# A scan and mixture-of-experts kernel: chunk scale from a Gram matrix, second round of slots after chunk 3, 163 output tiles, another order

## The chip, the cores and the metric

The kernel runs on one core of a Trainium2 chip. A core has TensorE (PE), VectorE (DVE), ScalarE (ACT), GpSimd (POOL) and SyncE (SP), which run their own instruction streams and meet at semaphores, and 16 DMA engines that move data between HBM and the two on-chip memories, SBUF and PSUM. The metric is the device time of one launch in microseconds; the time of a version is the median of its runs.

## The reference

A gated linear recurrence over 4 sequences of 5056 tokens with 256 features gives 20224 rows of 256 values. Each row goes to the one of 8 experts with the largest gate logit, through that expert's two-layer network, and is scaled by its softmax share and by a sigmoid.

```python
log_a = c * sig_r * np.log(np.clip(a_base, 1e-06, 1.0 - 1e-06))[None, None, :]
a_t = np.exp(log_a)
x_gated = np.sqrt(np.maximum(1.0 - a_t * a_t, 1e-06)) * sig_i * x
for t in range(S):
    h = a_t[:, t] * h + x_gated[:, t]
    y[:, t] = h
...
logits = x @ w_gate                    # x: the 20224 rows of y
e_idx = np.argmax(logits, axis=1)
for e in range(E):
    mask = e_idx == e
    h = np.maximum(x[mask] @ w1[e], 0.0)
    out[mask] = gate_w[mask, None] * eom[mask, e, None] * (h @ w2[e])
```

## The kernel before

Tokens come in 21 chunks: chunks 0 and 1 hold 4 tiles of 128 tokens each, chunks 2 to 19 hold 8, chunk 20 holds 6. For a chunk, in blocks of 4 tiles, SP loads the three inputs, ACT and DVE make decay and gated input, and DVE runs the scan (L685). Then the states are cut into two half-precision parts, which needs a power-of-two scale. In chunks 0 and 1 the states are turned into rows by PE (`project`, L719) and each row gets a scale of its own, from a maximum that DVE takes over the PSUM tile (`top`, L733 to L738). From chunk 2 on one scale serves the whole chunk: DVE takes the largest value per feature (`peak`, L771), spreads it over a diagonal (`spread`, L778 and L780), PE sends it to all partitions (`cast`, L784) and DVE makes the scale (`level`, L789 to L793). SP then turns the two parts into rows with a DMA transpose (`flip`, L823), PE computes logits (L831), DVE picks the expert and counts positions (L942), and POOL scatters each tile's rows to the experts' regions in HBM (`scatter_rows`, L427).

The expert network works in slots. A slot is 128 or 256 rows of one expert: SP fetches the rows transposed (L1073), PE runs the first layer into `ph` (L1129), ACT and DVE cut its output into two parts `h` (L1144, L1147), PE runs the second layer into `po` (L1186), ACT scales the result (L1198), POOL stores 128 rows per instruction (L1201). With three products per layer a slot of 128 rows is 48 matmuls of 128 columns and 24 of 256; a slot of 256 rows is 96 of 256 columns. The table SETS says after which chunk each expert gets a slot, and how wide: a *round* is the 8 slots of one chunk. An expert with fewer new rows than its slot holds takes old rows again, and these are not stored. Rows that are over after the last round go into ENDS slots of 128 rows, whose expert is found on the chip; should these not be enough, a loop adds 9 at a time.

The weights of an expert are loaded and cut into two parts by ACT and DVE (`unit`, L548 and L558) during the first chunks. Two Gram matrices per expert on PE (L507) give their scales.

PE, ACT and DVE get their instructions from a planner (`in_order`), which sorts the work by ranks and by assumed durations; the tables of ranks at the head of the file and the `time` arguments of `work` set the order, and each engine runs its own list strictly in that order. SP's and POOL's instructions are issued in the same order. From chunk 3 on a scatter also waits for the ReLU (L1144) that the planner put last before it, so that scatters are spread in time.

Of the kernel before, what the change touches and what calls it, by code (L numbers as in the profile page):

```python
# [7 lines left out]
F32 = mybir.dt.float32  # L8
# [9 lines left out]
P = 128  # L18
# [7 lines left out]
SETS = {1: 128, 2: 128, 4: 128, 5: 128, 6: 128, 8: 128, 9: 128, 10: 128, 11: 128, 13: 256, 15: 256, 17: 256, 19: 256}  # L26
# [5 lines left out]
ENDS = 29  # L32
# [22 lines left out]
LAG = 0.00132  # L55
ALONE = (0, 1, 3, 6)
QUICK = -11.495
ROOT = -24.122
EARLY = -672.359
UNIT_RANK = (509.634, 423.588, 415.962, -121.889, 422.863, 543.847, 40.166, 546.044, 522.559, 567.262, -167.684, 542.792, -125.616, -161.472, 40.642, -115.487)  # L60
CHUNK_RANK = (-672.139, -298.533, 527.534, 84.515, 462.374, 144.822, 553.848)
SLOT_RANK = (-52.797, -70.553, 319.009, -156.421, -51.418)
FILL = -114.953
LOAD_RANK = -17.21
# [158 lines left out]
def rglru_moe(ctx: ExitStack, tc: tile.TileContext, x, r_gate, i_gate, a_param, wg, wog, w1, w2, out, shape):  # L223
# [7 lines left out]
    assert D == 2 * P and E == 8 and F == 8 * P and N % P == 0 and N + (FILLS + 1) * P <= REGION and max(SETS.values()) <= FILLS * P  # L231
# [220 lines left out]
    undo = const.tile([P, 2, E], F32, name="undo")  # L452
# [6 lines left out]
    def unit(u, staged):  # L459
# [58 lines left out]
        def bits():  # L518
            pn = tiles["pg", u][:, P:P + 1]
            nc.vector.tensor_scalar(sc, pn.bitcast(I32), 25, 23, op0=ALU.logical_shift_right, op1=ALU.logical_shift_left)  # L520
            nc.vector.tensor_scalar(sc, sc, -1.0, float((168 - TOP, 172)[i] << 23), op0=ALU.mult, op1=ALU.add)
# [77 lines left out]
    def chunk(c):  # L599
# [102 lines left out]
        rused, row_at = [], []  # L702
        lows, flips = [], []
        for b in range(0, nt, 4) if c < BY_PE else ():
            nb = min(4, nt - b)
            iu = blocks[b // 4][6]
            group = []
            for j in range(b, b + nb):
                pool = "ps_h" if c < len(FIRST) and j % 4 > 1 else "ps_r"
                pu, pold = rings[pool].new()  # L710
                row_at.append(len(rings["rows"].tiles) % ROWS)
                used, old = rings["rows"].new()
                rused.append(used)

                def project(j=j, pool=pool):
                    pf = tiles["prow", c, j] = (ps_h if pool == "ps_h" else ps_r).tile([P, 512], F32, name=f"prow_{c}_{j}", tag=pool)
                    H = tiles["it", (c, j // 4 * 4)]
                    for h in range(ND):
                        nc.tensor.matmul(  # L719
                            pf[:, h * P:(h + 1) * P + 2 * E], lhsT=H[:, h, (j % 4) * P:(j % 4 + 1) * P],  # L720
                            rhs=iw[:, h, :], start=h == 0, stop=h == ND - 1, skip_group_check=True,
                        )

                def pr(j):
                    return tiles["prow", c, j][:, 0:ND * (P + 2 * E)].rearrange("p (h d) -> p h d", h=ND)[:, :, 0:P]

                def r4(j):
                    return rows_all[:, row_at[j], 0:META].rearrange("p (k h d) -> p k h d", k=2, h=ND)

                def top(js, pr=pr):  # L730
                    am, sc = st("am", 1), st("sc", 1, I32)
                    for j in js:
                        nc.vector.tensor_reduce(am[:, j, :], pr(j), axis=AX.XY, op=ALU.max, apply_absolute_value=True)  # L733
                    js = slice(js[0], js[-1] + 1)
                    nc.vector.tensor_scalar(
                        sc[:, js, :], am[:, js, :].bitcast(I32), 0x7F000000, 0x7F000000, op0=ALU.bitwise_and, op1=ALU.bitwise_xor
                    )
                    nc.vector.tensor_scalar(  # L738
                        sc[:, js, :], sc[:, js, :], float(TOP - 1 << 23), float(0x7F000000), op0=ALU.add, op1=ALU.min
                    )  # L740

                def hi(j=j, pr=pr, r4=r4):
                    sc = st("sc", 1, I32)[:, j, :].bitcast(F32)
                    if c < len(UPPERS) and UPPERS[c] == "D":
                        nc.vector.tensor_scalar(r4(j)[:, 0], pr(j), sc, None, op0=ALU.mult)
                    else:
                        nc.scalar.activation(r4(j)[:, 0], pr(j), AF.Copy, scale=sc)

                def lo(j=j, pr=pr, r4=r4):
                    nc.vector.tensor_copy(st("lz", 2 * E)[:, j, :], tiles["prow", c, j][:, P:P + 2 * E])  # L750
                    nc.vector.scalar_tensor_tensor(
                        r4(j)[:, 1], pr(j), st("sc", 1, I32)[:, j, :].bitcast(F32), r4(j)[:, 0], op0=ALU.mult, op1=ALU.subtract
                    )

                w = work("PE", 0.49, project, [states[b // 4], pold, gates], EARLY + c / 100, uses=[pu, iu], slack=SLACK[c > 4])
                group.append((j, w, pu, old, used, hi, lo))
                if len(group) == TOPS or j == b + nb - 1:
                    js = [v[0] for v in group]
                    t = work(
                        "DVE", 0.385 * len(js) + 0.22, lambda js=js, f=top: f(js), [v[1] for v in group] + chain["small"],  # L760
                        tail_rank + TAIL, uses=[v[2] for v in group],
# [79 lines left out]
        if c >= BY_PE:  # L841
# [6 lines left out]
            for blk in blocks:  # L848
                pus.append(rings["ps_r"].new())
# [422 lines left out]
    with tc.manual_schedule(engines=engines):  # L1272
        for w in in_order([w for w in works if not w.late], {"DVE": 3.0, "ACT": 3.0}):
            w.emit()
# [43 lines left out]
```

## Time and profile before

| | |
|---|---|
| median of 3 runs | 1047.06 us (1043.95 to 1047.54) |
| the profiled execution | 1041.86 us, span 1040.2 us |
| PE, weight loads | 945.2 us busy (91%), 871.8 us (84%) |
| DVE, ACT, POOL | 708.7 us (68%), 623.7 us (60%), 365.5 us (35%) |
| mean granted TensorE clock | 0.955 |

Busy time is an average over stages. Matmul and weight load overlap, so a busy PE is read as "PE had work", and what a slot costs is read from the distance between the same places of two slots that follow each other. The granted clock is a share of full speed: 1.0 is 2.4 GHz, 0.5 is 1.2 GHz.

### The profile page before, as it was taken

Reading aid. Unit: us, or ns where it says so; the run is one execution under the profiler, and the core shown is the slowest. Engines: PE = TensorE matmul, PEld = TensorE weight load, DVE = VectorE, ACT = ScalarE, POOL = GpSimd, SP = SyncE. Lnnn points to the kernel's source line nnn. Section 1 sums busy time; section 2 is a strip of 40 time slices with the busy share of each in tenths; the row PEclk is TensorE's granted clock in tenths of the full one; section 3 lists DMA queues with packets and bytes.
Section 4 is the critical chain, followed back from the end, with each engine's and each line's share of the span. In section 5 each row is a group of like instructions: output and inputs, shape, how many; then the busy total and the mean of one; then the engine's idle time right before and its main releaser. Section 6 shows DMA issues by size and latency. Waiting matters only on the chain.

```text
span 1040.2 us, 29569 instructions
## 1 busy us (share of the span) xinstructions
PE 945.2 (91%) x11462; PEld 871.8 (84%) x11462; DVE 708.7 (68%) x1798; ACT 623.7 (60%) x931; POOL 365.5 (35%) x341
## 2 busy tenths in 40 slices
PE   2449549999999989999999999999999999999996
PEld 2438449989989989899999888888888889999996
DVE  4988998999889888888888888885222222342231
ACT  6977886788678677768778788532232322333332
POOL 1120522553555444544445455443212122111111
PEclk8658869999999999999999999999999999999999
DMA  9997678999999999989999899766122212788971
GB/s 328 382 274 168 196 202 191 211 220 209 222 235 217 209 239 242 181 195 215 243 199 226 211 220 212 142 153 185 51 52 52 52 47 97 233 245 235 254 232 44
DMA packets 274447, 200.82 MB, mean 193 GB/s; under 512 B 213725, under 2 KB 224735, under 8 KB 274305
## 3 DMA queue, kind: packets, MB, share of 16 engines
q1 hardware_dynamic: 248224, 139.89, 59.3%
q0 software_dynamic: 15552, 42.23, 12.8%
q10 hardware_dynamic: 10528, 16.78, 4.7%
q8 instruction: 94, 1.54, 0.6%
q14 instruction: 49, 0.39, 0.2%
HBM read 79.09 MB, written 45.28 MB: 120 GB/s over the span
## 4 chain that ended last, share of the span: by engine, by line
PE 64%; issue 9%; DVE 7%; DMA 6%; ACT 3%; POOL 2%; SPq 1%; POOLq 0%; ACTq 0%; DVEq 0%
PE ph L1129 32%; PE po L1186 30%; DMA xt<-xs 3%; POOL out_dram L1201 2%; DMA xs<-rows_all,posi 1%; DMA rt<-in_r_gate_dram 1%; SPq L823 1%; PE lg L831 1%; DVE h L1147 1%; DVE it L685 1%; DVE rt L814 1%; ACT rt L807 1%; DMA it<-in_i_gate_dram 0%; ACT w1r L548 0%; DVE w1r L558 0%
## 5 line engine op out<-in xcount | busy, mean ns | idle before, releaser
L1186 PE MATMUL po<-w2r,h 128*128 128x256 f16 (+1 forms) x3960 | 557.5, 274 | 7.8 <-ACT h L1144 5.6
L1129 PE MATMUL ph<-xt,w1r 128*128 128x128 f16 (+1 forms) x4992 | 463.5, 238 | 20.8 <-DMA xt<-xs 11.2
L1129 PEld LDWEIGHTS <-w1r 128*128 128x128 f16 x4992 | 377.5, 99 | 47.9 <-issue 8.7
L1186 PEld LDWEIGHTS <-h 128*128 128x128 f16 x3960 | 362.5, 98 | 43.4 <-ACT h L1144 5.7
L1147 DVE SCALAR_TENSOR_TENSOR h<-ph,h 128x512 f16<-128x512 f32 x330 | 223.0, 684 | 239.8 <-ACT h L1144 238.7
L1201 POOL DMA_INDIRECT out_dram<-ot,osc x165 | 184.7, 1119 | 449.0 <-ACT ot L1198 402.7
L1144 ACT ACTIVATE h<-ph 128x512 f16<-128x512 f32 x330 | 192.5, 592 | 236.6 <-PE ph L1129 149.4
L427 POOL DMA_INDIRECT xs<-rows_all,posi x158 | 177.3, 1122 | 204.5 <-ACT h L1144 74.5
L1198 ACT ACTIVATE ot<-po,osc 128x256 f32<-128x256 f32 x165 | 74.0, 468 | 110.4 <-PE po L1186 103.9
L1129 PE MATMUL ph<-xt,ws 128*128 128x128 f16 x1392 | 106.1, 219 | 0.0
L685 DVE TENSOR_TENSOR_SCAN it<-rt,last,it 128x512 f32<-128x512 f32 (+4 forms) x78 | 95.9, 1240 | 0.6
L1129 PEld LDWEIGHTS <-ws 128*128 128x128 f16 x1392 | 92.4, 98 | 3.9
L642 ACT ACTIVATE rt<-rt,lam 128x512 f32<-128x512 f32 (+1 forms) x80 | 62.2, 802 | 0.6
L814 DVE SCALAR_TENSOR_TENSOR rt<-it,scale,rt 128x512 f16<-128x512 f32 (+1 forms) x76 | 50.2, 701 | 12.4 <-ACT rt L807 12.3
L654 DVE SCALAR_TENSOR_TENSOR it<-it,xt 128x1024 f32<-128x1024 f32 (+1 forms) x40 | 48.2, 1205 | 14.2 <-ACT it L651 14.1
L632 ACT ACTIVATE rt<-rt 128x1024 f32<-128x1024 f32 (+1 forms) x40 | 41.7, 1041 | 21.7 <-DMA rt<-in_r_gate_dram 21.6
L638 DVE SCALAR_TENSOR_TENSOR xt<-it,xt 128x1024 f32<-128x1024 f32 (+1 forms) x40 | 48.1, 1206 | 3.8 <-ACT it L635 3.7
L635 ACT ACTIVATE it<-it 128x1024 f32<-128x1024 f32 (+1 forms) x40 | 41.7, 1042 | 10.1 <-DMA it<-in_i_gate_dram 5.7
L646 ACT ACTIVATE it<-rt 128x1024 f32<-128x1024 f32 (+1 forms) x40 | 41.7, 1043 | 7.9 <-DVE xt L638 6.3
L771 DVE TENSOR_REDUCE peak<-it 128x1 f32<-128x1024 f32 (+1 forms) x38 | 45.4, 1197 | 0.0
L651 ACT ACTIVATE it<-it,quarter 128x1024 f32<-128x1024 f32 (+1 forms) x40 | 44.2, 1133 | 0.3
L807 ACT ACTIVATE rt<-it,scale 128x1024 f16<-128x1024 f32 (+1 forms) x38 | 41.1, 1128 | 3.2 <-DVE scale L793 3.1
(165 smaller groups left out, 562.2 us busy)
## 6 DMA issues: line engine op xcount, KB each, us to landing
ws<-w1r SPq DMA_DIRECT2D x58, 512.0 KB
rt<-in_r_gate_dram SPq DMA_DIRECT2D x39, 512.0 KB
it<-in_i_gate_dram SPq DMA_DIRECT2D x39, 512.0 KB
xt<-in_x_dram SPq DMA_DIRECT2D x39, 512.0 KB
w2r<-in_moe_w_dram ACTq DMA_DIRECT2D x7, 1024.0 KB
w1r<-in_moe_w_dram ACTq DMA_DIRECT2D x7, 1024.0 KB
out_dram<-ot,osc POOLq DMA_INDIRECT x165
xs<-rows_all,posi POOLq DMA_INDIRECT x158
```

What stands on the lines that cost most here:

```text
L427: op = nc.gpsimd.indirect_dma_start(out=xs[:, :], out_offset=bass.IndirectOffsetOnAxis(ap=pos, axis=0), in_=rows.bitcast(F32), in_offset=None,
L642: nc.scalar.activation(r[:, h], r[:, h], AF.Exp, scale=lam[:, h:h + 1], bias=lam[:, h:h + 1])
L654: nc.vector.scalar_tensor_tensor(t("it"), t("it"), 0.5e-3, t("xt"), op0=ALU.max, op1=ALU.mult)
L685: nc.vector.tensor_tensor_scan(H[:, h, lo:hi], A[:, h, lo:hi], H[:, h, lo:hi], first, op0=ALU.mult, op1=ALU.add)
L807: nc.scalar.activation(halves(key, 0, m // P), of_tiles(key, m), AF.Copy, scale=tiles["scale_of", c])
L814: nc.vector.scalar_tensor_tensor(halves(key, 1, m // P)[:, :, h], of_tiles(key, m)[:, :, h], tiles["scale_of", c], halves(key, 0, m // P)[ ...
L1129: nc.tensor.matmul(ph[:, i, 0:w], lhsT=ws[:, f // 2 % 2, a, c, f % 2 * P:(f % 2 + 1) * P], rhs=xt[:, b * ND + c, 0:w], start=k == 0, stop= ...
L1144: newest["relu"] = nc.scalar.activation(part(0, f0), tiles["ph", s, f0][:, :, 0:w], AF.Relu).ins
L1147: nc.vector.scalar_tensor_tensor(part(1, f0), tiles["ph", s, f0][:, :, 0:w], 0.0, part(0, f0), op0=ALU.max, op1=ALU.subtract)
L1186: nc.tensor.matmul(po[0:pw, j], lhsT=hh[:, a, f % 4, j * P:j * P + pw], rhs=second(b), start=f + j + a + b == 0, stop=f == NF - 1 and a == ...
L1198: nc.scalar.activation(ot[0:pw], tiles["po", s][0:pw, j], AF.Copy, scale=tiles["osc", s][0:pw, j, 0:1])
L1201: op = nc.gpsimd.indirect_dma_start(out=out[:, :], out_offset=bass.IndirectOffsetOnAxis(ap=tiles["osc", s][0:pw, j, 1:2].bitcast(I32), axi ...
```

## The change

- Chunks 0 to 3 get their scale from a Gram matrix: PE multiplies the upper halves of the states' words with themselves (`gram`, 8 products a block), DVE takes one maximum over the 128x128 result (`most`), PE sums it over the partitions (`energy`), and DVE makes the scale (`level`). In chunks 0 and 1 the scale is now one for the chunk.
- The second round moves from chunk 2 to chunk 3 and later rounds to other chunks: 8 rounds of 128 rows and 5 of 256 instead of 9 and 4. ENDS falls from 29 to 19. The tiles stored are 64 + 80 + 19 = 163 instead of 72 + 64 + 29 = 165.
- The scale that undoes the weights' comes from one integer addition instead of a reciprocal and a product.
- All ranks and some assumed durations have other values, so that every engine's order is another.

```diff
-SETS = {1: 128, 2: 128, 4: 128, 5: 128, 6: 128, 8: 128, 9: 128, 10: 128, 11: 128, 13: 256, 15: 256, 17: 256, 19: 256}
+SETS = {1: 128, 3: 128, 4: 128, 5: 128, 6: 128, 8: 128, 9: 128, 10: 128, 12: 256, 14: 256, 16: 256, 18: 256, 20: 256}
-ENDS = 29
+ENDS = 19
-CHUNK_RANK = (-672.139, -298.533, 527.534, 84.515, 462.374, 144.822, 553.848)
+CHUNK_RANK = (-855.378, -810.159, -966.965, 81.302, 66.372, -304.019, 2.418)
...
-                def top(js, pr=pr):
-                    am, sc = st("am", 1), st("sc", 1, I32)
-                    for j in js:
-                        nc.vector.tensor_reduce(am[:, j, :], pr(j), axis=AX.XY, op=ALU.max, apply_absolute_value=True)
...
+        def gram(key, m, first):
...
+            for j in range(0, m, P):
+                for h in range(ND):
+                    blk = upper[:, h, j:j + P, 1]
+                    nc.tensor.matmul(
+                        tiles["lg", c, 0][:, 272:272 + P], lhsT=blk, rhs=blk, start=first and j + h == 0, stop=False, skip_group_check=True,
                     )
+        def most():
+            em = tiles["em", c] = small.tile([P, 1], F32, name=f"em_{c}", tag="em")
+            nc.vector.tensor_reduce(em, tiles["lg", c, 0][:, 272:272 + P], axis=AX.X, op=ALU.max)
+
+        def energy():
+            nc.tensor.matmul(
+                tiles["lg", c, 0][:, 400:401], lhsT=ones32, rhs=tiles["em", c], start=False, stop=False, skip_group_check=True,
+            )
+
+        def level():
+            sc = small.tile([P, 1], I32, name=f"scale_{c}", tag="scale")
+            tiles["scale_of", c] = sc.bitcast(F32)
+            nc.vector.tensor_scalar(
+                sc, tiles["lg", c, 0][:, 400:401].bitcast(I32), 24, 23, op0=ALU.logical_shift_right, op1=ALU.logical_shift_left,
+            )
+            if c >= BY_PE:
...
+                nc.vector.tensor_scalar(inv, sc, float(61 - TOP << 23), None, op0=ALU.add)
+            nc.vector.tensor_scalar(sc, sc, -1.0, float(193 + TOP << 23), op0=ALU.mult, op1=ALU.add)
...
+        if c < GRAMS:
...
+            mo = work("DVE", 0.3, most, [gr] + chain["small"], late_rank, uses=[pu0])
+            en = work("PE", 0.25, energy, [mo], EARLY + c / 100, uses=[pu0], slack=SLACK[c > 4])
+            le = work("DVE", 0.3 + 0.15 * (c >= BY_PE), level, [en], late_rank, uses=[pu0])
+        else:
+            peaks = [
...
     def unscale(e):
-        nc.vector.reciprocal(undo[:, :, e:e + 1], wsc.bitcast(F32)[:, :, e:e + 1])
-        nc.vector.tensor_tensor(tab[:, 2, e:e + 1], undo[:, 0, e:e + 1], undo[:, 1, e:e + 1], op=ALU.mult)
+        nc.vector.scalar_tensor_tensor(
+            tab[:, 2, e:e + 1].bitcast(I32), wsq[:, 0, e:e + 1], float(41 + TOP << 23), wsq[:, 1, e:e + 1], op0=ALU.add, op1=ALU.add,
+        )
```

The first place is POOL's queue from the scatters of chunk 2 (`posi_2`) to the store of slot 7 (`ot_7`), the last slot of the first round. `x6` is six equal instructions. Before:

```order
L427 DMA xs_84<-rows_all_130,posi_2_1218 172032x264 x5
L1201 DMA out_0_dram<-ot_3_0_1411,osc_3_1269 20224x256
L427 DMA xs_84<-rows_all_130,posi_2_1218 172032x264 x3
L427 DMA xs_84<-rows_all_130,posi_3_1663 172032x264 x6
L1201 DMA out_0_dram<-ot_4_0_1760,osc_4_1708 20224x256
L427 DMA xs_84<-rows_all_130,posi_3_1663 172032x264 x2
L1201 DMA out_0_dram<-ot_5_0_1856,osc_5_1721 20224x256
```

The same place now:

```order
L428 DMA xs_84<-rows_all_130,posi_2_1115 172032x264 x8
L1227 DMA out_0_dram<-ot_2_0_1281,osc_2_1071 20224x256
L1227 DMA out_0_dram<-ot_3_0_1456,osc_3_1335 20224x256
L428 DMA xs_84<-rows_all_130,posi_3_1622 172032x264 x6
L1227 DMA out_0_dram<-ot_4_0_1778,osc_4_1732 20224x256
L428 DMA xs_84<-rows_all_130,posi_3_1622 172032x264 x2
L1227 DMA out_0_dram<-ot_5_0_1880,osc_5_1746 20224x256
```

The last two scatters of chunk 3 stand between the stores of slots 4 and 5 in both; before, no slot of the second round needed them, and now all eight do.

The second place is ACT around the last weights to be cut (`fw15`), up to the second ReLU of slot 4 (`h_4_1`). Before:

```order
L646 ACTIVATE it_4_4_1516<-rt_4_4_1265 128x1024
L651 ACT_TABLE_LOAD
L651 ACTIVATE it_4_0_1031<-it_4_0_1031,quarter_92 128x1024
L513 ACTIVATE dg_15_1673,sq_15_1674<-pg_15_1627 128x128
L651 ACTIVATE it_4_4_1516<-it_4_4_1516,quarter_92 128x1024
L548 ACTIVATE w2r_132<-fw15_0_1420,wsc_133 128x1024
L548 ACTIVATE w2r_132<-fw15_1_1567,wsc_133 128x1024
L632 ACT_TABLE_LOAD
L632 ACTIVATE rt_5_0_1587<-rt_5_0_1587 128x1024
L1144 ACTIVATE h_4_1_1700<-ph_4_4_1381 128x4x128
```

The same place now:

```order
L942 ACT_TABLE_LOAD
L942 ACTIVATE zs_3_1607<-zs_3_1607,inv_3_1448 128x8
L637 ACTIVATE it_5_0_1571<-it_5_0_1571 128x1024
L653 ACT_TABLE_LOAD
L653 ACTIVATE it_4_4_1530<-it_4_4_1530,quarter_92 128x1024
L514 ACTIVATE dg_15_1696,sq_15_1697<-pg_15_1655 128x128
L550 ACTIVATE w2r_132<-fw15_0_1517,wsc_133 128x1024
L550 ACTIVATE w2r_132<-fw15_1_1585,wsc_133 128x1024
L634 ACT_TABLE_LOAD
L634 ACTIVATE rt_5_0_1624<-rt_5_0_1624 128x1024
L634 ACTIVATE rt_5_4_1694<-rt_5_4_1694 128x1024
L1170 ACTIVATE h_4_1_1724<-ph_4_4_1303 128x4x128
```

The ReLU stands behind the same weights as before, with one gate more (`rt_5_4`) and, from the first ReLU of slot 0 on, seven table loads ahead of it instead of six.

The third place is DVE where chunk 1 gets its scale. Before:

```order
L733 TENSOR_REDUCE am_1_415<-prow_1_0_400 128x1
L733 TENSOR_REDUCE am_1_415<-prow_1_1_406 128x1
L735 TENSOR_SCALAR sc_1_416<-am_1_415 128x2
L738 TENSOR_SCALAR sc_1_416<-sc_1_416 128x2
L638 SCALAR_TENSOR_TENSOR xt_2_0_191<-it_2_0_187,xt_2_0_191 128x1024
L750 COPY lz_1_430<-prow_1_0_400 128x16
L751 SCALAR_TENSOR_TENSOR rows_all_130<-prow_1_0_400,sc_1_416,rows_all_130 128x256
```

The same place now:

```order
L717 TENSOR_REDUCE em_1_450<-lg_1_0_425 128x1
L560 SCALAR_TENSOR_TENSOR w1r_131<-w1r_131,wsc_133 128x4x256 x2
L727 TENSOR_SCALAR scale_1_481<-lg_1_0_425 128x1
L734 TENSOR_SCALAR scale_1_481<-scale_1_481 128x1
L560 SCALAR_TENSOR_TENSOR w2r_132<-w2r_132,wsc_133 128x2048
L826 COPY lz_1_509<-lg_1_0_425 128x16
L827 SCALAR_TENSOR_TENSOR rows_all_130<-lg_1_0_425,scale_1_481,rows_all_130 128x256
```

One reduction and two small operations a chunk take the place of four reductions and four small ones.

## Rows read from the trace of the kernel before

**Rows 1.** Windows: busy time of each engine by stage, granted clock, DMA share, GB/s.

```profile
0.00:150.00 150.00, 75.16 (x810) 68.10 (x810) 124.50 (x313) 119.41 (x158) 33.50 (x41) 0.74 0.88 265
150.00:170.00 20.00, 19.57 (x244) 17.62 (x245) 18.58 (x44) 12.37 (x21) 8.65 (x9) 0.87 0.52 134
170.00:545.00 375.00, 366.40 (x5152) 344.36 (x5150) 327.89 (x824) 283.96 (x406) 176.25 (x153) 0.99 0.98 218
545.00:720.00 175.00, 172.73 (x1733) 154.79 (x1731) 147.09 (x391) 113.14 (x172) 84.89 (x76) 1.00 0.84 198
720.00:1031.00 311.00, 311.00 (x3532) 286.80 (x3530) 90.68 (x229) 94.39 (x176) 61.25 (x63) 1.00 0.48 135
```

**Rows 2.** Chain that ended last: start, length, what; the same place of consecutive slots.

```profile
271.91 1.00 PE ph L1129 x18
...
277.21 1.00 PE ph L1129 x18
...
736.85 1.97 PE ph L1129 x18
...
747.32 1.97 PE ph L1129 x18
```

**Rows 3.** Groups of instructions, from the page.

```profile
L1201 POOL DMA_INDIRECT out_dram<-ot,osc x165 | 184.7, 1119 | 449.0 <-ACT ot L1198 402.7
L771 DVE TENSOR_REDUCE peak<-it 128x1 f32<-128x1024 f32 (+1 forms) x38 | 45.4, 1197 | 0.0
```

**Rows 4.** Groups by line, DVE: busy, mean ns of one.

```profile
L733 DVE TENSOR_REDUCE am<-prow 128x1 f32<-128x256 f32 x8 | 3.1, 417 | 0.7 <-PE prow L719 0.5
L735 DVE TENSOR_SCALAR sc<-am 128x2 int32<-128x2 int32 x4 | 0.7, 173 | 0.1
L789 DVE TENSOR_REDUCE scale<-lg 128x1 f32<-128x128 f32 x19 | 5.4, 282 | 0.3 <-PE lg L784 0.3
L790 DVE TENSOR_SCALAR scale<-scale 128x1 int32<-128x1 int32 x19 | 2.9, 154 | 0.7
L780 DVE TENSOR_SCALAR dp<-iw,peak 128x128 bf16<-128x128 f32 x19 | 6.0, 318 | 0.7
L1228 DVE RECIPROCAL undo<-wsc 128x2 f32<-128x2 f32 x8 | 1.3, 164 | 0.2
```

**Rows 5.** Timeline of PE: start, length, instruction, count, idle time before.

```profile
53.72 1.86 PE L507 MATMUL pg<-w2r 128*128 128x128 bf16 x16 [0.28 <-DVE wsc L520]
74.71 6.80 PE L1129 MATMUL ph<-xt,w1r 128*128 128x128 f16 x72 [5.83 <-DMA xt<-xs]
99.88 1.08 PE L507 MATMUL pg<-w1r 128*128 128x128 bf16 x16
150.31 2.40 PE L1186 MATMUL po<-w2r,h 128*128 128x256 f16 x9 [5.59 <-ACT h L1144]
212.76 4.18 PE L1129 MATMUL ph<-xt,w1r 128*128 128x128 f16 x72
387.38 2.72 PE L1129 MATMUL ph<-xt,w1r 128*128 128x128 f16 x24 [2.73 <-DMA xt<-xs]
```

**Rows 6.** Timeline of ACT.

```profile
145.23 2.17 ACT L548 ACTIVATE w2r<-fw,wsc 128x1024 f16<-128x1024 f32 x2
147.42 1.28 ACT L632 ACT_TABLE_LOAD   x1
148.72 1.06 ACT L632 ACTIVATE rt<-rt 128x1024 f32<-128x1024 f32 x1
149.68 1.55 ACT L1144 ACTIVATE h<-ph 128x512 f16<-128x512 f32 x3
169.22 0.47 ACT L1198 ACTIVATE ot<-po,osc 128x256 f32<-128x256 f32 x1 [3.29 <-PE po L1186]
```

**Rows 7.** Waits of ACT from 50 to 150 us: total, times, longest.

```profile
ACT it L635 <- DVE mx L881: 2.2, 1, 2.2
ACT it L646 <- DVE xt L638: 2.0, 2, 1.3
ACT w1r L548 <- DVE wsc L520: 1.6, 1, 1.6
```

**Rows 8.** Timeline of POOL and of SP.

```profile
63.03 0.97 POOL L427 DMA_INDIRECT xs<-rows_all,posi  x1 [0.30 <-issue]
69.02 1.30 SPq L1073 DMA_TRANSPOSE xt<-xs  x1
159.26 0.97 POOL L427 DMA_INDIRECT xs<-rows_all,posi  x1 [0.60 <-ACT h L1144]
199.89 0.97 POOL L427 DMA_INDIRECT xs<-rows_all,posi  x1 [0.30 <-issue]
202.77 5.03 SPq L823 DMA_TRANSPOSE rows_all<-rt  x1
208.85 2.21 SPq L1073 DMA_TRANSPOSE xt<-xs  x1
```

More of the change, by code (lines that the diff above doesn't have):

```diff
@@ L700, in st @@
             return tiles[nm, c]
[L702 to L728, printed above, removed]
-                def top(js, pr=pr):
-                    am, sc = st("am", 1), st("sc", 1, I32)
-                    for j in js:
-                        nc.vector.tensor_reduce(am[:, j, :], pr(j), axis=AX.XY, op=ALU.max, apply_absolute_value=True)
-                    js = slice(js[0], js[-1] + 1)
-                    nc.vector.tensor_scalar(
-                        sc[:, js, :], am[:, js, :].bitcast(I32), 0x7F000000, 0x7F000000, op0=ALU.bitwise_and, op1=ALU.bitwise_xor
-                    )
[L738 to L761, printed above, removed]
-                    )
-                    for j, w, pu, old, used, hi, lo in group:
-                        w = work("DVE" if c < len(UPPERS) and UPPERS[c] == "D" else "ACT", 0.41, hi, [t, old], tail_rank + TAIL, uses=[pu, used])
-                        lows.append(work("DVE", 0.5, lo, [w], tail_rank + TAIL, uses=[pu, used]))
-                    group = []
@@ L841, in chunk @@
         if c >= BY_PE:
-            late_rank = tail_rank + TAIL
-            peaks = [
-                work("DVE", 0.07 + 1.07 * blk[10], lambda b=blk[0], key=blk[4], m=blk[1] * P: peak(b, key, m), [states[blk[0] // 4]] + chain["small"], late_rank, uses=[blk[6]])
-                for blk in blocks
-            ]
-            pus = []
-            for blk in blocks:
-                pus.append(rings["ps_r"].new())
-            sp = work("DVE", 0.37, spread, peaks, late_rank)
-            ca = work("PE", 0.1, cast, [sp, pus[0][1]], EARLY + c / 100, uses=[pus[0][0]], slack=SLACK[c > 4])
-            le = work("DVE", 0.87, level, [ca], late_rank, uses=[pus[0][0]])
             for blk, (pu, pold) in zip(blocks, pus):
@@ L1149, in slot @@
             hu, hold = hus[f0 // 4]
-            m = work("ACT", 0.11 + 0.2125 * g * scale, relu, [m, hold], rank, uses=[pu, hu])
-            evac += [work("DVE", 0.08 + 0.265 * g * scale, low, [m], rank, uses=[pu, hu])] * (g // 2)
+            m = work("ACT", 0.13 + 0.2125 * g * scale, relu, [m, hold], rank, uses=[pu, hu])
+            evac += [work("DVE", 0.095 + 0.265 * g * scale, low, [m], rank, uses=[pu, hu])] * (g // 2)
         ou, oold = rings["osc"].new()
@@ L1272, in rglru_moe @@
     with tc.manual_schedule(engines=engines):
-        for w in in_order([w for w in works if not w.late], {"DVE": 3.0, "ACT": 3.0}):
+        for w in in_order([w for w in works if not w.late], {"DVE": 1.7, "ACT": 0.8}):
             w.emit()
```

138 lines of the change are left out of this document (100 added, 38 removed).

## The prediction

> **What bounds the kernel now.** I read the windows by stage first [rows 1]. Two regimes can be seen. Until 150 us PE is busy for 75.16 of 150.00 us, at a mean granted clock of 0.74 (a mixture of 1.2 and 2.4 GHz), while DVE is busy for 124.50 and ACT for 119.41: the weights are being cut into parts and the first chunks prepared. From then on PE has nearly no gap: 366.40 of 375.00 us from 170 to 545, 172.73 of 175.00 from 545 to 720, and 311.00 of 311.00 from 720 to 1031, with the clock at 0.99 to 1.00. So behind 150 us the time is the sum of PE's work and of 8.6 + 2.3 = 10.9 us of holes, and ahead of it the time is whatever lets PE start its dense stretch.
>
> That start is read next, in the timeline of PE [rows 5]. At 150.31 PE goes on with the second layer of slot 4 after 5.59 us idle, and the releaser is ACT's `h`. I call this moment T0. On ACT [rows 6] that ReLU (149.68) stands behind the last weights to be cut (145.23), a table load (147.42) and a gate (148.72). From 50 to 150 us ACT itself waited for DVE, in its three largest waits, for 2.2 + 2.0 + 1.6 = 5.8 us [rows 7].
>
> Last comes the chain of waits, for the price of a slot [rows 2]. The same place of consecutive 128-row slots lies at 271.91 and 277.21: 5.30 us a slot. For 256-row slots it lies at 736.85 and 747.32: 10.47.
>
> The profiled execution took 1041.86 us: span 1040.2 and 1.7 around it. The median is 1047.06, so 5.2 is added at the end to go from the one to the other.
>
> **Term A, the slots: -11.6 us.** Before, 9 rounds of 8 slots and 29 at the end are 101 narrow slots, with 4 x 8 = 32 wide ones: 101 + 64 = 165 stores, which is the count in the page [rows 3]. Now there are 8 x 8 + 19 = 83 narrow and 5 x 8 = 40 wide: 163. On PE 101 x 5.30 + 32 x 10.47 = 870.3 becomes 83 x 5.30 + 40 x 10.47 = 858.7. It is on the path, since PE has no gap there. Two 128-row slots less would be 10.6; the other 1.0 comes from 16 narrow slots becoming 8 wide ones (2 x 5.30 - 10.47 = 0.13 each). The 19 are enough only if every expert's rows fit. I counted the rows per expert from the reference's inputs: what is left after the last round is 0, 122, 353, 140, 66, 524, 606 and 161 rows, thus 0 + 1 + 3 + 2 + 1 + 5 + 5 + 2 = 19 slots of 128. It fits, with none over.
>
> At this price a rule of the Trainium skill can be weighed. The rows show 18 first-layer matmuls of 128 columns in 1.00 us, 55.6 ns each [rows 2]. "TensorE: Matmul & The Clock Gate", section "Back-to-back issue gap", gives about 81 ns for each matmul of 128 columns in a sustained stream of weight loads and matmuls, and calls the lower figure that of an isolated one. Narrow slots would then cost more against wide ones: 48 x (81 - 55.6) = 1.2 us a slot, an estimate from that page, and 18 narrow slots fewer would bring some 22 us more. This trace disagrees, since its weight loads run beside the matmuls and 55.6 is what it measures in the stream; I give it under one in a hundred, within the relief case below.
>
> **Term B, the Gram products on PE: 0.** Chunks 0 to 3 have 1 + 1 + 2 + 2 = 6 blocks with 8 products each, 48 matmuls. Sixteen Gram matmuls of the weights took 1.86 us at the low clock and 1.08 at the high one [rows 5], so 48 take 3.2 to 5.6. They fall into the first 150 us, where PE is idle half the time [rows 1], and they drop the spreading products of chunks 2 and 3. If that cover is gone, that is, if they stand on PE ahead of a ReLU's input at T0, up to +5.
>
> **Term C, DVE and T0: -2 us.** The work that DVE loses [rows 3, 4]: in chunks 0 and 1, 8 x 0.417 + 4 x 2 x 0.173 = 4.7 us become 2 x (0.282 + 2 x 0.154) = 1.2. The reduction over the Gram matrix isn't in the trace; `scale` from a 128x128 tile (282 ns) is its nearest row. In chunks 2 and 3, four `peak` of 1.197 and twice a spreading of 0.318, a reduction of 0.282 and five small operations of 0.154 make 7.5; now 2 x (0.282 + 3 x 0.154) = 1.5. The undoing scale goes from two operations of 164 ns to one, for 8 experts: -1.3. Together 3.5 + 6.0 + 1.3 = 10.8 us less on DVE ahead of T0, where it was busy for 124.50 of 150.
>
> But T0 hangs on ACT, which loses no operation. The order shows one table load more (1.28) and one gate more (1.06) ahead of the same ReLU [rows 6], +2.3. So the relief of DVE counts only as far as ACT waited for DVE, 5.8 us in the rows shown and a little more in smaller waits. Between -7.5 (all waits gone and the two additions hidden in others) and +4 (none gone, the additions in full, and half of the 3.2 to 5.6 us of Gram products in the way), I take -5.8 + 2.3 = -3.5 cut to -2, since some of the 5.8 will come back as another wait, of ACT for inputs that now arrive no sooner (DMA is at 0.88 of its time there).
>
> **Term D, a new hole at the second round: +4 us.** Before, that round needed chunk 2, whose last scatters stand far ahead. Now it needs chunk 3. Its last scatter was issued at 159.26, held back on purpose behind a ReLU [rows 8], 9.0 us after T0. In POOL's order it stands between the stores of slots 4 and 5, as before. From a last scatter to the first matmul of that chunk's round it took 11.7 us in chunk 1 (63.03 to 74.71, with a fetch at 69.02 [rows 5, 8]) and 12.9 in chunk 4 (199.89 to 212.76, with a 5.03 us transpose of the next chunk's states between it and the fetch at 208.85 [rows 5, 8]). So the second round can start 20.7 to 21.9 us after T0. The first round's work ends sooner: slot 7's output was scaled at 169.22 [rows 6], 18.9 after T0, with some of the second round's matmuls already among it. The hole is 2 to 3 us. The row at 387.38 shows what follows one: after 2.73 us idle, 24 matmuls took 2.72 us, 113 ns each, the 1.2 GHz level, where 24 x 55.6 ns = 1.33 would do [rows 5]. That is +1.4, and about +4 together. From below: 0, if chunk 3 is ready earlier against T0, as its maxima's 6.0 us on DVE would allow. From above: 9, if another 5.03 us transpose stands in the way.
>
> **Term E: 0.** The other holes, 10.9 us, stay as they are: in POOL's order the second round begins four slots after the store ahead of its chunk's last scatter, the third five, as before, and all later ones seven or more, as before. They cannot give more than 10.9, and the row at 387.38 puts a price of about 4.1 on each that is added.
>
> **Sum.** -11.6 + 0 - 2 + 4 + 0 = -9.6: 1041.86 goes to 1032.3 for a profiled execution, and the median from 1047.06 to about 1037. Lower end: A with C's -7.5 and no hole, -19.1, 1028. Upper: A with C at +4 and D at 9, +1.4, 1048.5.
>
> **Rivals.**
> Relief: the DVE work removed carries through to T0, and chunk 3 is ready in time. For it: DVE at 124.50 of 150. Against it: the ReLU at T0 waits on ACT's own queue [rows 6]. Time: 1047.06 - 19.1 = 1028.
>
> Gain eaten: T0 is later by the additional ACT work and the hole is near its upper bound; -11.6 + 2 + 8 = -1.6, about 1045. For it: ACT is at 119.41 of 150 and gets more. Against it: ACT's waits for DVE leave room.
>
> Starved second round, the slower one: chunk 3 is not ready near T0 + 20 but one chunk's preparation later, because the new order lets it queue on DVE behind the weights' last parts. Its price: the last scatters of chunks 3 and 4 lie 199.89 - 159.26 = 40.6 us apart [rows 8], PE-bound and paced, so being late by one chunk is at most that; I take half of it as the likely size, 20 us with the matmuls at the lower clock behind it: 1047.06 - 11.6 + 20 = 1055. It decides from a hole of 11.6 + 5.2 = 16.8 us on. Against it: all eight scatters stand ahead of slot 5's store in POOL's order, as before.
>
> Slots not enough: should the regrouping leave more than 19 slots, the loop adds nine, 9 x 5.30 = 47.7, and the time is 1047.06 - 9.6 + 47.7 = 1085: the change would not do what its table says. Against it stands the count above.
>
> **How the numbers follow.** The forecast gets 0.60, with a range of its own of 1033 to 1042; relief 0.13; gain eaten 0.18; starved 0.07; slots not enough 0.02. No change means within 0.5%, 5.2 us, which is what a measurement of this kernel can tell. Faster (below 1041.8): 0.58 of the forecast, all of relief, 0.02 of gain eaten: 0.73. Same: 0.02 of the forecast, 0.155 of gain eaten and 0.015 of starved (holes under 16.8), 0.19. Slower: the other 0.055 of starved, 0.02 of slots not enough and 0.005 of gain eaten, 0.08. The range that holds 8 in 10 is 1028 to 1049.
>
> **What the profile after would show.** Term A: 163 stores, and 5.30 and 10.47 between consecutive slots. Term B: Gram rows at 67 to 116 ns each, in stretches where PE would be idle. Term C: DVE some 11 us less busy up to T0, and slot 4's second ReLU 0 to 4 us earlier. Term D: PE idle once for 2 to 9 us ahead of the first `ph` of the second round, released by the DMA that fetches `xt`, and a few matmuls at the lower clock behind it. Term E: idle time of PE behind that of 9 to 13 us. The forecast is wrong if the hole is over 10 us, if T0 moves by more than 5 us either way, or if slots have another period.

## The result, and the profile after

The changed kernel takes 1031.93 us (median of 4 runs, 1031.38 to 1031.99) against 1047.3 for the kernel before (4 runs, 1043.95 to 1049.23): a ratio of 0.9855 with a 95% interval of 0.983 to 0.9881, 15.4 us less. The forecast was 1037 within 1028 to 1049; the time lies in that range, but 1 us below the 1033 to 1042 that the forecast case had for itself. The sign and the largest term were right; the gain was 5 us larger than forecast, and two smaller terms were wrong, one in its sign.

Its profiled execution took 1031.38 us, span 1029.6. The windows of the stages that [rows 1] shows of before (the columns are those: length, busy time of PE, weight loads, DVE, ACT and POOL, granted clock, DMA share, GB/s), and two more, cut where PE's dense stretch starts and ends:

```profile
0.00:150.00 150.00, 77.35 (x864) 70.93 (x864) 117.06 (x288) 116.87 (x156) 33.30 (x40) 0.76 0.91 263
150.00:170.00 20.00, 15.85 (x207) 13.96 (x208) 17.22 (x42) 14.54 (x22) 8.16 (x9) 0.83 0.60 150
170.00:545.00 375.00, 365.04 (x4971) 339.08 (x4969) 321.75 (x802) 289.42 (x410) 168.50 (x153) 1.00 0.97 215
545.00:720.00 175.00, 174.35 (x1747) 156.27 (x1746) 151.10 (x407) 122.72 (x182) 82.20 (x73) 1.00 0.83 199
...
0.00:153.11 153.11, 77.35 (x864) 70.94 (x865) 120.17 (x290) 119.97 (x160) 34.62 (x41) 0.76 0.91 264
153.11:1021.20 868.09, 856.44 (x10124) 784.31 (x10124) 572.62 (x1436) 515.81 (x779) 322.07 (x297) 1.00 0.72 172
```

The same cut in the trace of the kernel before:

```profile
0.00:150.31 150.31, 75.16 (x810) 68.10 (x810) 124.81 (x314) 119.72 (x159) 33.50 (x41) 0.74 0.88 265
150.31:1031.37 881.06, 870.06 (x10652) 803.66 (x10652) 583.92 (x1485) 503.55 (x772) 331.05 (x299) 0.99 0.77 183
```

A span is now a sum of four parts: T0, PE's busy time from T0 to its last matmul, its idle time in that stretch (length less busy time), and the tail. Before: 150.31 + 870.06 + 11.00 + 8.83 = 1040.2. After: 153.11 + 856.44 + 11.65 + 8.40 = 1029.6. So T0 went up by 2.8, work down by 13.6, holes up by 0.65, the tail down by 0.4: -10.6 in this pair of executions. All further comparisons are made with these four parts.

PE's timeline after, at T0, at the second round and at the largest later hole; the first and the last row answer to those at 150.31 and 387.38 in [rows 5], and the 48 matmuls at 172.02 are the first layer of the second round's first slot:

```profile
153.11 0.61 PE L1212 MATMUL po<-w2r,h 128*128 128x256 f16 x2 [6.57 <-ACT h L1170]
...
172.02 2.84 PE L1155 MATMUL ph<-xt,w1r 128*128 128x128 f16 x48
175.90 1.51 PE L1155 MATMUL ph<-xt,w1r 128*128 128x128 f16 x24 [1.04 <-DMA xt<-xs]
...
357.32 2.52 PE L1155 MATMUL ph<-xt,w1r 128*128 128x128 f16 x42 [1.73 <-DMA xt<-xs]
```

POOL and SP around the second round, as in [rows 8]:

```profile
161.56 0.97 POOL L428 DMA_INDIRECT xs<-rows_all,posi  x1 [0.31 <-issue]
162.91 5.05 SPq L863 DMA_TRANSPOSE rows_all<-rt  x1
168.69 1.21 SPq L1099 DMA_TRANSPOSE xt<-xs  x1
```

Chunk 3's last scatter goes 8.45 us after T0, the 5.05 us transpose of the next chunk stands between it and the fetch, and still the round's first matmuls run at 172.02, 10.5 us behind the scatter and 18.9 behind T0, when the first round ends. A hole of 1.04 is left, ahead of the round's second slot, and the 24 matmuls behind it take 1.51, 63 ns each: the clock did not fall (granted 1.00 from 175.9 to 178.0).

The stores at the end of the kernel (163 in all) give the periods of wide and of narrow slots: 10.48 between 853.21 and 863.69, 5.30 between 992.87 and 998.17, as before.

```profile
853.21 0.98 POOL L1227 DMA_INDIRECT out_dram<-ot,osc  x1 [8.21 <-ACT ot L1224]
...
863.69 0.98 POOL L1227 DMA_INDIRECT out_dram<-ot,osc  x1 [8.21 <-ACT ot L1224]
...
992.87 0.98 POOL L1227 DMA_INDIRECT out_dram<-ot,osc  x1 [3.84 <-DVE osc L1186]
998.17 0.98 POOL L1227 DMA_INDIRECT out_dram<-ot,osc  x1 [4.32 <-DVE osc L1186]
```

### The profile page after: what moved, and what is told of

Same layout as the page of the kernel before. It is cut to its first block, busy times and chain, and to the rows that moved or that the text cites. A ratio compares the mean times of both kernels' runs of the same rounds, so it can differ in the third digit from the quotient of the medians.

```text
span 1029.6 us, 28136 instructions
## 1 busy us (share of the span) xinstructions
PE 933.8 (91%) x10988; PEld 855.2 (83%) x10988; DVE 692.8 (67%) x1725; ACT 636.2 (62%) x939; POOL 357.7 (35%) x339
## 3 DMA queue, kind: packets, MB, share of 16 engines
q0 software_dynamic: 15456, 42.22, 13.3%
## 5 line engine op out<-in xcount | busy, mean ns | idle before, releaser
L1212 PE MATMUL po<-w2r,h 128*128 128x256 f16 (+1 forms) x3912 | 532.8, 273 | 9.1 <-ACT h L1170 6.6
L1155 PE MATMUL ph<-xt,w1r 128*128 128x128 f16 (+1 forms) x4992 | 470.4, 241 | 11.1 <-DMA xt<-xs 9.8
L1155 PEld LDWEIGHTS <-w1r 128*128 128x128 f16 x4992 | 382.4, 98 | 41.6 <-issue 7.3
L1170 ACT ACTIVATE h<-ph 128x512 f16<-128x512 f32 x326 | 190.4, 592 | 261.2 <-PE ph L1155 195.0
L1227 POOL DMA_INDIRECT out_dram<-ot,osc x163 | 177.9, 1091 | 413.1 <-ACT ot L1224 269.0
L1224 ACT ACTIVATE ot<-po,osc 128x256 f32<-128x256 f32 x163 | 71.9, 466 | 50.9 <-PE po L1212 47.4
L1155 PE MATMUL ph<-xt,ws 128*128 128x128 f16 x912 | 68.4, 219 | 0.0
L1155 PEld LDWEIGHTS <-ws 128*128 128x128 f16 x912 | 59.9, 98 | 2.4
L637 ACT ACTIVATE it<-it 128x1024 f32<-128x1024 f32 (+1 forms) x40 | 41.7, 1042 | 21.2 <-DMA it<-in_i_gate_dram 21.0
L648 ACT ACTIVATE it<-rt 128x1024 f32<-128x1024 f32 (+1 forms) x40 | 41.8, 1044 | 13.3 <-DVE xt L640 11.9
L739 DVE TENSOR_REDUCE peak<-it 128x1 f32<-128x1024 f32 (+1 forms) x34 | 40.6, 1196 | 0.0
```

The source lines that it names most:

```text
L1155: nc.tensor.matmul(ph[:, i, 0:w], lhsT=ws[:, f // 2 % 2, a, c, f % 2 * P:(f % 2 + 1) * P], rhs=xt[:, b * ND + c, 0:w], start=k == 0, stop= ...
L1170: newest["relu"] = nc.scalar.activation(part(0, f0), tiles["ph", s, f0][:, :, 0:w], AF.Relu).ins
L1212: nc.tensor.matmul(po[0:pw, j], lhsT=hh[:, a, f % 4, j * P:j * P + pw], rhs=second(b), start=f + j + a + b == 0, stop=f == NF - 1 and a == ...
L1224: nc.scalar.activation(ot[0:pw], tiles["po", s][0:pw, j], AF.Copy, scale=tiles["osc", s][0:pw, j, 0:1])
L1227: op = nc.gpsimd.indirect_dma_start(out=out[:, :], out_offset=bass.IndirectOffsetOnAxis(ap=tiles["osc", s][0:pw, j, 1:2].bitcast(I32), axi ...
```

## The experiments

### Both kernels once more

> The kernel before, unchanged, once more, to see what differs between its executions: the profiled one of it took 1041.86 us, the four timed ones 1043.95 to 1049.23, while the five of the changed kernel lie within 1031.38 to 1031.99. Theory: the difference is inside the span, in the holes ahead of rounds whose fetches come late (2.73 us at 387.38 and 2.44 at 442.18 in the first trace, each with matmuls at the lower clock behind it); then a slower execution shows a longer span, with 1.7 us around it as before, and a trace of it has holes or low-clock stretches of 2 to 7 us more behind 150 us. Rival 1: the span is 1040 again and the rest lies around it (over 3 us between span and time). Rival 2: the start differs, that is the first `po` of the dense stretch lies 2 to 7 us later than 150.31, and what follows is the same. 1042 to 1049 by all three.

33 executions of the kernel before on one chip went from 1040.4 to 1051.18 us, with a mean of 1045.2; only three were under the 1041.86 of the first trace. Span and time differed by 1.7 in every one, so the differences lie inside. The new trace has a span of 1043.7 = 150.74 + 868.56 + 15.52 + 8.88: the start is the same, and the holes are 4.5 us longer. The two places of the first trace, 387.38 and 442.18, were now:

```profile
391.84 2.74 PE L1129 MATMUL ph<-xt,w1r 128*128 128x128 f16 x24 [4.95 <-DMA xt<-xs]
...
445.73 2.18 PE L1129 MATMUL ph<-xt,w1r 128*128 128x128 f16 x36 [1.79 <-DMA xt<-xs]
```

One hole is 4.95 instead of 2.73, the other 1.79 instead of 2.44, and four more fetches came late by 0.52 to 1.49. So in this pair of traces the theory holds and both rivals fall: fetches of rows that come now earlier, now later, change the length of the kernel before. That they make the whole of the 1040 to 1051 is not shown by two traces. Its first profiled execution was one of the shortest.

> The changed kernel, unchanged, once more, beside the kernel before on the same chip: the chip of the last four runs gave the kernel before 1055.6 us and showed waits of PE for nothing that the profile names (14 to 19 us of them, against 0 to 1.3 in the first traces). Theory (each chip adds its own time to both kernels, the gain stays): 12 to 16 us below the kernel before on the same chip, with the start at 153 where PE has no such waits. Rival (the gain depends on the chip, since the changed kernel loses more to such waits): under 5 us below it where these waits show.

On the third chip of these experiments (the first is that of the runs above, the second the one that the expectation speaks of): 1030.99 us (1030.25 to 1033.96) against 1045.02 for the kernel before, a ratio of 0.9872 (0.9844 to 0.99), 14.0 us less. The span of 1028.5 is 152.60 + 856.25 + 10.95 + 8.70. Against the trace of before_again this is +1.9, -12.3, -4.6 and -0.2. No waits without a name showed here beyond 1.3 us, so this run could not tell theory from rival; one of the experiments below does.

### The table of rounds alone

```diff
-SETS = {1: 128, 2: 128, 4: 128, 5: 128, 6: 128, 8: 128, 9: 128, 10: 128, 11: 128, 13: 256, 15: 256, 17: 256, 19: 256}
-ENDS = 29
+SETS = {1: 128, 3: 128, 4: 128, 5: 128, 6: 128, 8: 128, 9: 128, 10: 128, 12: 256, 14: 256, 16: 256, 18: 256, 20: 256}
+ENDS = 19
```

> The kernel before with only the new table of rounds and 19 end slots; scales from maxima and all ranks as before. Theory: slots are worth -11.6 us on PE, the second round then waits for chunk 3 (hole of 1 to 4 us), the start of the dense stretch stays within 3 us of 150.3: 1047.3 - 11.6 + 2 = about 1038 (1034 to 1042), and about 10 us of the 15.4 gained come from this table alone. Rival (the order matters more than the slots): ranks that were not made for this table give new holes of 8 us and more behind 150 us, and the time stays at 1043 or above. Rival (the Gram scales carry the gain): the same, 1043 or above, but with the hole ahead of the second round over 10 us, since chunk 3's maxima are on DVE.

This edit of the kernel before made it slower: 1050.57 us (1045.35 to 1053.61) against 1044.1 on the same chip, ratio 1.0069 (1.0046 to 1.0093). Its trace has 165.60 + 856.20 + 12.48 + 9.32 = 1043.6. The work fell by 13.9 as the slots promise, the holes rose by 1.5, and T0 went up by 15.3. This profiled execution, 1045.35, is the shortest of the eight; the other 5 us of the median are in no trace. The planner, with ranks made for another table, put more preparation of chunk 4 ahead of the last weights: DVE's first rows up to 165 us show six `peak` instead of four and 14 scans instead of 11.

```profile
L685 DVE TENSOR_TENSOR_SCAN it<-rt,last,it 128x512 f32<-128x512 f32 x14 | 17.3, 1274 | 0.1
...
L771 DVE TENSOR_REDUCE peak<-it 128x1 f32<-128x1024 f32 x6 | 7.3, 1211 | 0.0
```

DVE is busy for 138.0 us up to T0, 13.2 more than before, and ACT waits 8.9 us for DVE's halves of the weights there. The first rival said what happened (the order takes the gain back), though not where: the loss is ahead of T0, not behind 150 us.

> The changed kernel with the old table of rounds and 29 end slots; Gram scales and new ranks stay. Theory: +11.6 us for the slots, -1.0 for the hole ahead of the second round, which needs chunk 2 again: 1031.9 + 10.6 = 1042.5 (1040 to 1046). Then Gram scales, ranks and the smaller holes are worth about 5 us of the 15.4. Rival (slots are the whole gain): 1046 to 1049, like the kernel before. Rival (ranks or Gram scales are the gain): under 1038.

The reverse edit of the changed kernel: 1051.05 us (1049.78 to 1053.62), ratio to before 1.0077 (1.0054 to 1.01), higher than any case expected. Its trace: 154.98 + 869.72 + 14.44 + 8.86 = 1048.0. The work is that of the old table again, 13.3 more than in the changed kernel; T0 is 1.9 later and the holes are 2.8 longer than in the first trace after. Under either order, then, the table is worth 13 to 14 us of PE's work, and a table under an order that was not made for it costs 5 to 17 us in the start and the holes.

### Gram scales and DVE

```diff
-GRAMS = 4
+GRAMS = 2
```

> The changed kernel with Gram scales in chunks 0 and 1 alone; chunks 2 and 3 take theirs from maxima again, which gives DVE about 6.0 us of work back ahead of the last weights. Theory (the start of the dense stretch hangs on ACT, and chunk 3 is ready only just in time for the second round): the start moves by under 2 us, the hole of 1.0 ahead of the second round grows by 0 to 3, and the time is 1032 to 1036. Rival (DVE's relief reaches the end one to one): 1037.5 to 1039, with the start 4 to 6 us later or the hole that much longer. Rival (no effect of the Gram scales at all): within 1 us of 1031.9.

1036.33 us (1028.48 to 1039.14); span 157.41 + 856.80 + 11.32 + 8.37 = 1033.9. This ran on the chip of before_again, where the changed kernel itself was not run; its ratio to before is 0.9903 (0.9868 to 0.9938) against the 0.9855 of the changed kernel. T0 is 4.3 later than in the trace after, with DVE busy for 125.69 up to it instead of 120.17. In the second round PE waits 2.65 us for a fetch, ahead of the fourth slot. The time lies between the two cases and the start at the rival's, so the start does not hang on ACT alone, unless the order, which differs too, did it. The next run keeps the order.

```diff
-            nc.vector.tensor_reduce(em, tiles["lg", c, 0][:, 272:272 + P], axis=AX.X, op=ALU.max)
+            for _ in range(11 if c in (2, 3) else 1): nc.vector.tensor_reduce(em, tiles["lg", c, 0][:, 272:272 + P], axis=AX.X, op=ALU.max)
```

> The changed kernel in the same order of instructions, with ten more maxima over the 128x128 Gram result in each of chunks 2 and 3, which nothing uses: 20 x 0.282 = 5.6 us of work back on DVE ahead of the last weights, about what the Gram scales took from it there. Theory (DVE's relief reaches the start of PE's dense stretch, since ACT waits for DVE there and PE for both): the start moves from 153.1 to 155 to 158 and the time to 1034 to 1037. Rival (ACT alone sets the start, as the prediction had it, and the 157.4 of the run with Gram scales in two chunks came from its other order): the start moves by under 1 us, 1031 to 1033.

This and the three runs with it fell on a chip on which the kernel before takes 1055.6 us: 1062.22 here, T0 at 167.34. Without the changed kernel beside it the run was only a hint, so it was repeated:

> 5.6 us of idle maxima back on DVE in chunks 2 and 3, same order, once more beside the changed kernel on one chip. The last trace had the start at 167.3 where the sisters with other edits had 160.6 to 162.2. Theory (DVE's relief reaches the start nearly one to one): start 4 to 7 us behind that of the changed kernel on this chip, time 4 to 8 us over it. Rival (ACT alone sets the start): within 1.5 us of it.

1037.7 us (1036.27 to 1039.3) beside 1030.99 of the changed kernel: +6.7. The added reductions in its trace, and T0 in the changed kernel's beside it and here:

```profile
L717 DVE TENSOR_REDUCE em<-lg 128x1 f32<-128x128 f32 x24 | 7.0, 291 | 2.7 <-PE lg L711 1.8 <-PE lg L807 0.2
```

```profile
152.60 0.61 PE L1212 MATMUL po<-w2r,h 128*128 128x256 f16 x2 [6.56 <-ACT h L1170]
...
160.23 0.61 PE L1212 MATMUL po<-w2r,h 128*128 128x256 f16 x2 [6.57 <-ACT h L1170]
```

20 more of them at 0.291 are 5.8 us, and T0 is 7.6 later than the 152.60 beside it; work and holes are the same within 1.2 (856.78 and 12.13). These maxima ahead of T0 reach the end in full: ACT alone does not set the start.

The way they take can be read from the waits up to T0 (columns: total, times, longest). In the changed kernel beside it:

```profile
ACT h L1170 <- PE ph L1155: 5.7, 2, 4.9
...
ACT rt L644 <- PE po L1212: 0.5, 1, 0.5
...
PE lg L720 <- DVE em L717: 1.1, 1, 1.1
```

With the added maxima:

```profile
ACT h L1170 <- PE ph L1155: 11.0, 4, 6.1
...
ACT rt L644 <- PE po L1212: 3.2, 1, 3.2
...
PE lg L720 <- DVE em L717: 5.6, 3, 2.6
```

ACT's waits for PE, all lines together, grew from 11.0 to 18.7 us, by as much as T0 moved, while its waits for DVE stayed as they were (5.2 and 5.1). PE waited longer for the maximum `em`, and ACT longer for PE. The added maxima stand in the chain that makes a chunk's scale; what the same time would cost elsewhere in DVE's list is not shown.

### ACT ahead of the start

```diff
-                by_scale(hi_by, d[:, 0], fw)
+                for _ in range(3 if u == 15 and k == 1 else 1): by_scale(hi_by, d[:, 0], fw)
```

> The changed kernel in the same order, with the upper part of the last quarter of the last expert's second weights written three times instead of once on ACT, right ahead of the ReLU that starts PE's dense stretch: 2 x 1.1 = 2.2 us more on ACT. Theory (a later start costs the end one to one, since PE has no reserve behind it): start 155.3, time 1034.1 (1033.5 to 1035). Rival (a later start is partly given back, since fetches that came late are then ready): the start moves by 2.2 but the time by under 1.2.

1056.22 us on the slow chip (T0 162.19), with nothing to compare it to; again beside the changed kernel:

> 2.2 us more on ACT right ahead of the ReLU that starts the dense stretch, same order, once more beside the changed kernel on one chip. Theory (the start is carried to the end one to one): 1.7 to 2.8 us over the changed kernel in the start and in the time. Rival (partly given back): start 2.2 later, time under 1.2 over it.

1034.29 us (1034.0 to 1036.21), +3.3, and T0 at 155.58, +3.0:

```profile
155.58 2.40 PE L1212 MATMUL po<-w2r,h 128*128 128x256 f16 x9 [8.93 <-ACT h L1170]
```

By the medians the theory holds, a little above its bounds: a later start is carried to the end. The trace is of the longest of the four, 6.0 over the changed kernel's; besides T0 its work is 4.1 more (860.37) and its holes 0.9 less (10.03), so it does not show this by itself.

```diff
-                ins = queue(WEIGHTS_BY, {"SP": nc.sync, "ACT": nc.scalar}[WEIGHTS_BY].dma_start(
+                ins = queue("SP" if u == 5 else WEIGHTS_BY, (nc.sync if u == 5 else nc.scalar).dma_start(
```

This edit tries a loss that the trace after shows on ACT, where before had 0.98 us idle ahead of the same gate:

```profile
22.25 0.38 ACTq L482 DMA_DIRECT2D w2r<-in_moe_w_dram  x1
22.68 1.06 ACT L634 ACTIVATE rt<-rt 128x1024 f32<-128x1024 f32 x1 [6.33 <-DMA it<-in_i_gate_dram]
```

> The changed kernel with one load of weights (second layer of expert 2) issued from SP instead of ACT, at the same place among the others. In the changed kernel's trace ACT stands still from 16.3 to 22.3 us at that issue, which waits for an earlier load to land, with the gates of the first chunks queued behind it; the kernel before had a wait of 1 us there. Theory (this early loss is why the start of the dense stretch is at 153.1 and not at 150 or less): ACT's gap at 16 us shrinks to 1 to 3 us, the start comes 2 to 5 us earlier, 1027 to 1030. Rival (what is won early is lost again in later waits of ACT for DVE and for loads): the start moves by under 1 us, 1031 to 1033.

> One load of weights issued from SP instead of ACT, once more beside the changed kernel on one chip. In the last trace ACT's gap at 16 us shrank from 6.3 to 4.3 us, and a new wait of 2.1 for DVE came at 47 us. Theory as it stands now (the early loss of ACT reaches the start by what is not lost again): start 0.5 to 2 us earlier than in the changed kernel on this chip, time 0.5 to 2 us below it. Rival (nothing is left of it): both within 0.5.

Beside the changed kernel it took 1032.72 us (1031.44 to 1037.96), 1.7 more, with T0 at 153.03 against 152.60. ACT's gap at 16 us fell from 6.33 to 4.53, and a new wait of 1.83 for DVE at 48.80 took it back. The theory falls, and what the rival says of the start holds: what this edit won was lost again. The 4.53 us that are left of the gap were not tested. The profiled execution, 1037.96, is the longest of the five, with work 3.7 and holes 3.9 above the changed kernel's (859.95 and 14.86).

The kernel with one load moved also tells how the gain depends on the chip. On the third chip its ratio to the kernel before is 0.9873 (0.9849 to 0.9898); on the slow one it was 0.9994 (0.9973 to 1.0014), nothing, and the three other edits of the changed kernel, two of which add work, came out between 0.9975 and 1.0061 on that chip. There the trace of the kernel with one load moved has T0 at 160.63, 860.71 of work and 19.36 of holes, and these waits of PE for nothing that the profile names (columns: total, times, longest), none of which the same kernel shows on the third chip:

```profile
PE pg L517 <- issue: 7.5, 2, 3.9
...
PE ph L1155 <- issue: 5.7, 13, 1.1
...
PE po L1212 <- issue: 1.7, 6, 0.4
```

So the rival of after_again has its case in this kernel with one load moved: on the chip where PE waits in this way the gain is gone. That these waits are the reason is not shown: the 7.5 us of `pg` lie ahead of T0, near 120 us, where PE is idle half the time, and the two others are 7.4. The kernel before has no trace on that chip, and the changed kernel itself wasn't run there, so why the new order loses more of it stays open.

### Scatters not held back

```diff
-        if c >= PACED[0] and "relu" in newest:
+        if c > PACED[0] and "relu" in newest:
```

> The changed kernel in the same order, with chunk 3's scatters no longer held behind ReLUs (those of later chunks still are). Theory (the second round's hole hangs on chunk 3's last scatter at 161.56): the scatter goes 2 to 6 us earlier, the 1.04 us hole at 175.90 goes, 1030 to 1031.5. Rival (the hole hangs on the fetch, which stands behind the 5.05 us transpose of chunk 4's states at 162.91): scatters earlier, hole and time the same within 0.6.

1053.99 us on the slow chip, 0.9975 of before (0.9951 to 0.9999). T0 was 161.94, and the last scatter of chunk 3 went at 169.98, 8.0 behind it instead of 8.45: the store of slot 4, which stands ahead of it in POOL's queue, holds it as the ReLU did. Neither case can be told from this run, since the scatter moved by only 0.4 against T0 and no hole for a fetch showed at the second round.

## Why the prediction was right and where it failed

**Term A, slots, -11.6: right, and a little low.** Work fell by 13.6 in the first pair, by 12.3 in the second, and by 13.9 and 13.3 when the table alone was changed under either order. The periods are what the sum used, 5.30 and 10.48. The surplus lies in matmuls at 1.2 GHz: before, 24 in 2.72 us at 387.38 and 36 in 3.73 at 442.18 cost 1.4 + 1.7 = 3.1 more than at 55.6 ns each (granted clock 0.51 and 0.57 there); after, none behind the second round ran so slowly. That would make 14.7; 1.1 of it I cannot place. In before_again the second of the two ran fast (36 in 2.18), and its work is 1.5 less. The 81 ns a matmul of "Back-to-back issue gap" (the Trainium skill, "TensorE: Matmul & The Clock Gate") are refuted by the measurement here: a narrow slot's 48 first-layer and 24 wider second-layer matmuls fit into 5.30 us.

**Term B, Gram products on PE, 0: right.** The 48 products took 4.8 us inside the bounds of 3.2 to 5.6, in the time when PE is idle half.

**Term C, T0, -2: wrong in sign, and in its reason.** T0 came 2.8 (2.3 in the second trace) later. The step that failed is "the relief of DVE counts only as far as ACT waited for DVE". With the order held fixed, 5.8 us on DVE moved T0 by 7.6, more than one to one, and 2.2 on ACT by 3.0. DVE's time came to T0 by way of PE, for which ACT waited 7.7 us longer, and not by ACT's waits for DVE, which did not grow. The largest wait of ACT in the window of [rows 7] was one for PE, and the sum left it out:

```profile
ACT h L1144 <- PE ph L1129: 8.3, 4, 4.7
```

The 2.3 us that ACT was to get more did not come either: up to T0 it is busy for 119.72 us before and 119.97 after, and both traces have 15 table loads ahead of T0's ReLU. The one more behind slot 0's first ReLU is one fewer ahead of it.

Part of the relief was used up by what DVE does ahead of T0. Up to the ReLU, before and after:

```profile
L685 DVE TENSOR_TENSOR_SCAN it<-rt,last,it 128x512 f32<-128x512 f32 x11 | 13.6, 1270 | 0.0
...
L654 DVE SCALAR_TENSOR_TENSOR it<-it,xt 128x1024 f32<-128x1024 f32 x7 | 8.5, 1219 | 4.5 <-ACT it L651 4.5
```

```profile
L687 DVE TENSOR_TENSOR_SCAN it<-rt,last,it 128x512 f32<-128x512 f32 x14 | 17.4, 1273 | 0.2
...
L656 DVE SCALAR_TENSOR_TENSOR it<-it,xt 128x1024 f32<-128x1024 f32 x8 | 9.8, 1224 | 6.4 <-ACT it L653 6.4
```

The new order puts three more scans and one more product there, 5.1 us, so of the 10.8 taken off DVE its busy time up to T0 shows only 124.81 - 120.17 = 4.6. Its idle time up to T0 grew by more, from 25.5 to 32.9, which makes T0 2.8 later. Most of this came in the first 50 us (33.45 us busy there before, 26.94 after). DVE's first scan runs 8.2 us later, in the trace before and after:

```profile
22.56 2.34 DVE L685 TENSOR_TENSOR_SCAN it<-rt,it 128x512 f32<-128x512 f32 x2
```

```profile
30.79 1.22 DVE L687 TENSOR_TENSOR_SCAN it<-rt,it 128x512 f32<-128x512 f32 x1
```

The load moved to SP brought it to 28.80, and these 2.0 us were lost again later; the other 6.2 were not tested, and why T0 is later stays open. I had counted the relief and not what the order moves into its place.

**Term D, hole at the second round, +4: too large, and not where it was forecast.** Ahead of the round's first slot neither trace after shows a wait for its fetch; the 1.04 of the first trace stand ahead of the second slot, and the second trace has none. Mis-sized was the lag from the last scatter to the first matmul: at most 10.5 us, where the two rows used gave 11.7 and 12.9. The second of these could not size it: at 212.76 PE had no idle time ahead of it [rows 5], so PE's own work may have made it that long. With so short a hole the price of the lower clock, 1.4, fell away too.

**Term E, other holes unchanged: wrong for the median.** In the first pair it held (holes +0.65 with D's). But the kernel before has holes that change from run to run, 11.0 in one trace and 15.5 in the other, while the two traces after have 11.65 and 10.95. That the new order is free of this is not shown: edits of it in the same order have 10.03 to 14.86 on the third chip. So how much of the 15.4 us the holes gave is open.

**The step from trace to median failed most.** I added the 5.2 us between the first profiled execution and the median of before to both kernels. That distance was chance: the execution was one of the shortest of the kernel before, and the changed kernel's two profiled ones differ from the medians beside them by under 1. So the forecast for a profiled execution, 1032.3, was met by 1031.38, and that was partly luck: C was 4.8 too low, D and E together 3.4 too high, A gave 2.0 more than forecast, and these nearly cancel. The median came out 5 lower than forecast.

Of the rivals, "relief" came nearest by its time (1028), for another reason than it gave; "gain eaten" is what the slow chip shows of the kernel with one load moved, by another cause; the starved round and too few end slots did not happen.

## What to carry to other kernels

Split a span at the moment when the bounding engine becomes dense, and compare start, work and holes apart: the work could be counted from slots here, the other two could not. Before the waits of one engine for another are taken as a bound, look whether it also waits for a third that hangs on the other. An order that a planner derives from ranks belongs to the table that it was made with: the table alone, and everything but the table, made this kernel slower, and only both together faster. And before a distance between a trace and a median is carried over to the changed kernel, look at how far the runs of before lie apart.

## What was not expected of the hardware

A hole of PE that waits for a fetch changes from run to run by over 2 us at the same place of the same kernel (2.73 and 4.95), and one kernel can be 1.3% faster than another on one chip and the same on the next, where PE shows some 15 us of waits that no semaphore explains, half of them ahead of T0 (0.9873 and 0.9994 of before, for the changed kernel with one load moved).
